# A wider gate on one load, a second bank for the last output tile, and one query tile turned a unit earlier, in a fused attention and feed-forward kernel

## The chip, the cores and the metric

The kernel runs on one core of a Trainium2 chip. The metric is the device time of one execution in microseconds (us). It was measured 13 times, and one execution was profiled. Times inside the kernel are counted from the first instruction of the profiled execution. PE is TensorE, DVE is VectorE, ACT is ScalarE, POOL is GpSimd, and SP is the engine that issues most of the DMA transfers.

## What is computed

Two stages follow each other. The first is a linear attention with a positional weight, over 8 batches of 8 heads, 576 positions and 64 channels:

```
phi(x) = concat(relu(x) * cos(theta_s), relu(x) * sin(theta_s))     # 64 -> 128 features
kv     = phi(k)^T v            z = sum_s phi(k)                      # per batch and head
x      = phi(q) kv / (phi(q) z + 1e-6)                               # attention output
```

The output is laid out as 4608 tokens of 512 channels and goes into a gated feed-forward block with 1536 hidden channels:

```
out = (gelu(x @ w_gate) * (x @ w_val)) @ w_out
```

All inputs and the output are float32. The kernel multiplies in bfloat16.

## The kernel before

**Stages and tiles.** The whole order is written out by hand: each engine carries out its own instructions in the order in which the program names them, and waits are put in where two instructions touch the same data or the same bank of PSUM. Positions of a batch are spread over the partitions so that a load is two transfers. `load` (L75) first issues the odd partitions (1, 3, ... 127; 4 positions each), then the even ones (0, 2, ... 126; 5 positions each):

```
for i, (s, r0, n) in enumerate(((1, 5, 4), (0, 0, 5))):
    (even if even and i == 1 else nc.sync).dma_start(
        out=dst[s:128:2, h0:h1, 0:n]..., in_=runs[:, :, r0:r0 + n]...)
```

For a whole batch the odd transfer of q is 512 KB and the even one 640 KB. There is one buffer each for raw q, k and v (`qf`, `kf`, `vf`), so the load of the next batch waits until the current one has been scaled into `qp`, `kp` and `vx`.

**Attention of a batch.** `sq` and `sk` scale q and k (ACT or DVE), `q_by_pe` turns a tile of q on PE, `kv_half` forms kv for four heads, `numer` (L190) multiplies one tile of 128 queries (8 matmuls into two banks) and normalises the result on DVE (`norm`: three instructions). `x_by_pe` (L318) then turns the normalised tile by 4 PE transposes into one bank, and ACT or DVE copies it into `xT`, the feed-forward input.

**Feed-forward.** `gv_unit(n, jt, c0, w, gb, vb)` (L209) does hidden tile `jt` of block `n` for `w` tokens from `c0`: 4 gate matmuls into bank `gb`, the gelu on ACT, 4 value matmuls into bank `vb`, and the product on DVE into `hT`. Block 0 is batch 0; blocks 1 to 8 hold 512 tokens each. `o_tile` multiplies 128 tokens of `hT` with `w_out` (12 matmuls into one bank), and ACT copies the result out for the store.

**Weights.** They are float32 in memory and are cast on their way by transfers that POOL issues. The first pair, hidden tiles 0 and 1 of gate and value (`load_w(0, 2)`, L345), is issued once batch 0's q has landed; tiles 2 and 3, 4 to 7 and 8 to 11 follow, then the two halves of `w_out` (L406, L407). After these, in the order of the program, stands a one-element copy by POOL (L408), and behind it the loads of batch 1 (`load_q(1)`, L409, and k and v). The copy reads the last element of the first half of `w_out` and writes an element of `qf`: it can only run once that half has landed, and a load that writes the same element has to wait for the copy.

**The start of block 1.** While the last output tiles of block 0 are multiplied, batch 1's attention tiles y0 to y4 are formed, turned, and given to the first two hidden tiles in pieces of 128, 128 and 256 tokens (L460 to L475). The piece of 256 tokens reads query tiles 2 and 3.

**The end.** The last of the 36 output tiles is done by `o_last` (L257) in two halves of 256 columns. For each half there are 12 matmuls; ACT copies the first 128 columns and DVE the second 128 (L267, L268), and SP and ACT issue one store each (L269, L270). It is called with bank 5.

Of the kernel before, what the change touches and what calls it, by code (L numbers as in the profile page):

```python
# [16 lines left out]
def kernel(  # L17
# [10 lines left out]
    nc = tc.nc  # L28
# [4 lines left out]
    C = H * D  # L33
# [24 lines left out]
    wo_sb = sb.tile([128, JT, C], BF16, name="wo_sb")  # L58
    xT = sb.tile([128, CT, N_TOK], BF16, name="xT")
    qf = sb.tile([128, H, NJ + 1, D], FP32, name="qf")  # L60
# [104 lines left out]
    def numer_mm(b, t, bank, g):  # L165
        for h in range(4 * g, 4 * g + 4):
            nc.tensor.matmul(  # L167
                ps[:, bank + g, (h % 4) * (D + 1):(h % 4 + 1) * (D + 1)],
                lhsT=qT[b % 2][:, t, h, :],
                rhs=kv[b % 2][:, h, 0:D + 1],  # L170
                start=True, stop=True,
            )

    def norm(xb, bank, g0, g1):

        n = g1 - g0
        nd = ps[:, bank + g0:bank + g1, 0:4 * (D + 1)].rearrange("p g (h e) -> p g h e", e=D + 1)
        den = rot.tile([128, 2, 4], FP32, name="den")
        nc.vector.tensor_scalar(den[:, 0:n], nd[:, :, :, D], EPS, None, op0=ALU.add)
        rec = rot.tile([128, 2, 4], FP32, name="rec")  # L180
        nc.vector.reciprocal(rec[:, 0:n], den[:, 0:n])
        nc.vector.tensor_tensor(  # L182
            xb[:, g0:g1], nd[:, :, :, 0:D],
            rec[:, 0:n, :, None].to_broadcast([128, n, 4, D]), op=ALU.mult,
        )

    def new_xb():
        return rot.tile([128, 2, 4, D], BF16, name="xb", bufs=4)

    def numer(b, t, bank):  # L190

        numer_mm(b, t, bank, 0)
        numer_mm(b, t, bank, 1)
        xb = new_xb()
        norm(xb, bank, 0, 2)
        return xb
# [12 lines left out]
    def gv_unit(n, jt, c0, w, gb, vb, mid=()):  # L209

        p0 = starts[n] + c0
        for ct in range(CT):
            nc.tensor.matmul(  # L213
                ps[:, gb, 0:w], lhsT=wg_sb[:, ct, jt * 128:(jt + 1) * 128],
                rhs=xT[:, ct, p0:p0 + w], start=(ct == 0), stop=(ct == CT - 1),
            )
        gel = rot.tile([128, 512], FP32, name="gel", bufs=3)
        nc.scalar.activation(gel[:, 0:w], ps[:, gb, 0:w], AF.Gelu)  # L218
        for f in mid:
            f()  # L220
        for ct in range(CT):
            nc.tensor.matmul(  # L222
                ps[:, vb, 0:w], lhsT=wv_sb[:, ct, jt * 128:(jt + 1) * 128],
                rhs=xT[:, ct, p0:p0 + w], start=(ct == 0), stop=(ct == CT - 1),
            )
        nc.vector.tensor_mul(hT[n % 2][:, jt, 64 + c0:64 + c0 + w], gel[:, 0:w], ps[:, vb, 0:w])  # L226
# [6 lines left out]
    def rows_ap(P, n):  # L233

        b, r = divmod(P, S)
        j, p0 = divmod(r, 128)
        rows = out[b * S:(b + 1) * S, :].rearrange("(i r) c -> i r c", r=9)
        if j < NJ:
            return rows[p0 // 2:(p0 + n) // 2, j:j + 6:5]
        return rows[:, NJ]  # L240
# [16 lines left out]
    def o_last(m, bank):  # L257

        c0 = 128 * m - starts[NB - 1] + 64
        o_sb = rot.tile([128, C], FP32, name="o_sb", bufs=4)  # L260
        for c in (0, 256):
            for jt in range(JT):
                nc.tensor.matmul(  # L263
                    ps[:, bank, c:c + 256], lhsT=hT[(NB - 1) % 2][:, jt, c0:c0 + 128], rhs=wo_sb[:, jt, c:c + 256],
                    start=(jt == 0), stop=(jt == JT - 1),
                )
            nc.scalar.copy(o_sb[:, c:c + 128], ps[:, bank, c:c + 128])  # L267
            nc.vector.tensor_copy(o_sb[:, c + 128:c + 256], ps[:, bank, c + 128:c + 256])  # L268
            nc.sync.dma_start(out=rows_ap(128 * m, 64)[:, :, c:c + 256], in_=o_sb[0:64, c:c + 256])  # L269
            nc.scalar.dma_start(out=rows_ap(128 * m + 64, 64)[:, c:c + 256], in_=o_sb[64:128, c:c + 256])  # L270
# [23 lines left out]
    def load_q(b):  # L294
        load(qf, q, b)
# [22 lines left out]
    def x_by_pe(b, t, xb, bank, eng, c0=0, c1=CT):  # L318
        p0 = b * S + t * 128
        cp = nc.vector.tensor_copy if eng == "v" else nc.scalar.copy  # L320
        xb2 = xb.rearrange("p g h d -> p (g h d)")
        view = ps[:, bank, 0:256].bitcast(BF16).rearrange("p (c t) -> p c t", c=CT)
        for ct in range(c0, c1):
            nc.tensor.transpose(out=view[:, ct], in_=xb2[:, ct * 128:(ct + 1) * 128], identity=ident)
        if t < NJ:
            cp(xT[:, c0:c1, p0:p0 + 128], view[:, c0:c1])  # L326
        else:
            cp(xT[:, c0:c1, p0:p0 + 64], view[:, c0:c1, 0:128:2])
# [76 lines left out]

    nc.gpsimd.dma_start(out=wo_sb[:, 0:6], in_=wo_r[:, 0:6])  # L406
    nc.gpsimd.dma_start(out=wo_sb[:, 6:12], in_=wo_r[:, 6:12])  # L407
    nc.gpsimd.tensor_copy(qf[0:1, 0, 0, 0:1], wo_sb[0:1, 5, C - 1:C])  # L408
    load_q(1)  # L409
    load_k(1)  # L410
    load(vf, v, 1, 0, 4)
# [55 lines left out]
    gv_unit(1, 1, 0, 128, 1, 5)  # L467
    x_by_pe(1, 2, y2, 6, "s")
    gv_unit(1, 0, 128, 128, 0, 4)
    gv_unit(1, 1, 128, 128, 1, 5)  # L470
    x_by_pe(1, 3, y3, 7, "s")
    y4 = numer(1, 4, 2)
    gv_unit(1, 0, 256, 256, 0, 4)
    x_by_pe(1, 4, y4, 6, "v")
    gv_unit(1, 1, 256, 256, 1, 5)  # L475
# [56 lines left out]
    for i, m in enumerate(last[:-1]):  # L532
        o_tile(NB - 1, m, 4 + i % 2)
    o_last(last[-1], 4 + (len(last) - 1) % 2)


# [28 lines left out]
```

## Time and profile before

| | us |
|---|---|
| median of 13 runs | 339.25 |
| lowest and highest of them | 335.4, 340.86 |
| the profiled execution's own time | 340.41 |
| its span, first to last instruction | 338.4 |
| PE busy in the span | 321.0 (95%) |
| DVE, ACT, POOL busy | 177.3, 149.8, 21.5 |
| mean granted PE clock | 0.988 |

The profile gives each engine's busy time, the same in 40 equal slices of the span, the busy share of the DMA engines, the waits (which engine at which line waited for whom, in total, how often, and the longest), the timeline, and the chain of work that ended last. "DMA share" can pass 1, since packets of different queues overlap on an engine. A PE that reads as busy isn't always at full rate: the granted clock is a row of its own.

### The profile page before, as it was taken

How to read it: one execution, taken by the hardware profiler on the slowest of the kernel's cores; microseconds unless marked ns; L12 is line 12 of the kernel's file. 1: busy time of each engine (PE TensorE's matmuls, PEld its weight loads, DVE VectorE, ACT ScalarE, POOL GpSimd, SP SyncE). 2: the span in 40 equal slices, each digit the busy share in tenths (PEclk: the TensorE clock that was granted, in tenths of full speed). 3: DMA queues.
4: the chain of work that ended last, by engine and by line, in shares of the span. 5: the costliest groups of instructions: out<-in, count | busy, mean ns of one | idle time of the engine just before them, and what ended most of it. 6: DMA issues, size and time to landing. Idle time of an engine off the chain costs nothing.

```text
span 338.4 us, 5911 instructions
## 1 busy us (share of the span) xinstructions
PE 321.0 (95%) x2225; PEld 172.7 (51%) x2260; DVE 177.3 (52%) x394; ACT 149.8 (44%) x275; POOL 21.5 (6%) x39
## 2 busy tenths in 40 slices
PE   7758999999999999999999999999999999999994
PEld 3546886665444544454445444544454444444443
DVE  4835459776766456645764576457645323222210
ACT  5834448775355325532553256225622332322321
POOL 2550001000010001000100010001000100000000
PEclk9969999999999999999999999999999999999999
DMA  7899984999939992997299829991914121000024
GB/s 232 236 206 207 233 290 120 363 197 351 164 61 159 369 182 48 198 370 164 42 225 367 138 44 195 374 174 32 202 35 75 32 62 33 31 31 33 32 63 93
DMA packets 84380, 54.65 MB, mean 162 GB/s; under 512 B 49408, under 2 KB 79872, under 8 KB 84352
## 3 DMA queue, kind: packets, MB, share of 16 engines
q1 hardware_dynamic: 78128, 49.10, 58.4%
q0 software_dynamic: 5792, 4.72, 8.8%
q10 hardware_dynamic: 432, 0.46, 0.4%
q8 instruction: 17, 0.28, 0.3%
q14 instruction: 11, 0.09, 0.1%
HBM read 37.75 MB, written 9.44 MB: 139 GB/s over the span
## 4 chain that ended last, share of the span: by engine, by line
PE 82%; DVE 6%; DMA 4%; issue 2%; ACT 2%; POOL 1%; SPq 1%; DVEq 0%; ACTq 0%; POOLq 0%
PE ps L245 27%; PE ps L213 25%; PE ps L222 24%; DVE vx L138 3%; PE ps L167 2%; DMA wv_sb<-in_moe_w_val_dram 2%; PE ps L151 2%; DMA qf<-in_q_dram 2%; DVE hT L226 1%; DVE xb L182 1%; PE ps L310 1%; PE ps L263 1%; ACT kp L134 1%; POOL wg_sb L291 1%; ACT xT L326 1%
## 5 line engine op out<-in xcount | busy, mean ns | idle before, releaser
L226 DVE TENSOR_TENSOR hT<-gel,ps 128x512 bf16<-128x512 f32 (+4 forms) x128 | 77.0, 603 | 135.1 <-PE ps L222 128.0
L213 PE MATMUL ps<-xT,wg_sb 128*128 128x512 bf16 (+5 forms) x498 | 114.1, 347 | 4.7 <-ACT xT L326 1.7
L222 PE MATMUL ps<-xT,wv_sb 128*128 128x512 bf16 (+5 forms) x500 | 112.8, 348 | 2.0 <-DMA wv_sb<-in_moe_w_val_dram 1.9
L218 ACT ACTIVATE gel<-ps 128x512 f32<-128x512 f32 (+4 forms) x128 | 67.8, 530 | 89.4 <-PE ps L213 86.6
L245 PE MATMUL ps<-wo_sb,hT 128*128 128x512 bf16 x413 | 95.3, 379 | 0.6
L222 PEld LDWEIGHTS <-wv_sb 128*128 128x128 bf16 x512 | 49.5, 99 | 47.3 <-DMA wv_sb<-in_moe_w_val_dram 2.1
L213 PEld LDWEIGHTS <-wg_sb 128*128 128x128 bf16 x512 | 47.4, 99 | 43.7 <-issue 2.5
L245 PEld LDWEIGHTS <-hT 128*128 128x128 bf16 x420 | 40.2, 98 | 45.8
L274 ACT COPY o_sb<-ps 128x512 f32<-128x512 f32 x35 | 20.5, 585 | 75.9 <-PE ps L245 71.7
L182 DVE TENSOR_TENSOR xb<-ps,rec 128x512 bf16<-128x512 f32 (+1 forms) x41 | 27.8, 678 | 1.5
L134 ACT ACTIVATE kp<-kf,sin_c 128x512 bf16<-128x512 f32 (+1 forms) x41 | 25.3, 679 | 0.9 <-DMA kf<-in_k_dram 0.9
L132 DVE TENSOR_SCALAR qp<-qf,cos_c 128x512 bf16<-128x512 f32 (+1 forms) x45 | 21.0, 511 | 0.8 <-DMA qf<-in_q_dram 0.8
L167 PEld LDWEIGHTS <-qT 128*128 128x128 bf16 x320 | 15.4, 99 | 8.8 <-issue 1.8
L134 ACT ACTIVATE qp<-qf,sin_c 128x512 bf16<-128x512 f32 (+1 forms) x30 | 18.8, 670 | 0.3 <-DMA qf<-in_q_dram 0.3
L132 DVE TENSOR_SCALAR kp<-kf,cos_c 128x512 bf16<-128x512 f32 (+1 forms) x45 | 18.0, 452 | 1.5 <-DMA kf<-in_k_dram 1.5
L167 PE MATMUL ps<-kv,qT 128*128 128x65 bf16 x320 | 17.1, 195 | 0.9 <-DVE kv L163 0.2
L206 POOL COPY xT<-xr 128x256 bf16<-128x256 bf16 x6 | 2.4, 400 | 205.7 <-DMA xr<-xb 205.7
L151 PEld LDWEIGHTS <-kp 128*128 128x128 bf16 x320 | 11.1, 97 | 3.5 <-issue 2.3
L151 PE MATMUL ps<-vx,kp 128*128 128x65 bf16 x320 | 11.9, 193 | 0.5
L138 DVE CAST vx<-vf 128x1280 bf16<-128x1280 f32 (+1 forms) x14 | 12.1, 892 | 0.3 <-DMA vf<-in_v_dram 0.3
L124 PE MATMUL ps<-junk 128*128 128x512 bf16 x30 | 9.5, 462 | 1.8 <-DVE par_i L101 1.7
L231 POOL COPY hT<-hT 128x768 bf16<-128x768 bf16 x8 | 7.6, 946 | 42.6 <-DVE hT L226 42.6
(53 smaller groups left out, 94.0 us busy)
## 6 DMA issues: line engine op xcount, KB each, us to landing
out_dram<-o_sb SPq DMA_DIRECT2D x38, 128.0 KB, 2.4
qf<-in_q_dram SPq DMA_DIRECT2D x7, 640.0 KB, 6.1
kf<-in_k_dram SPq DMA_DIRECT2D x7, 640.0 KB, 7.6
out_dram<-o_sb SPq DMA_DIRECT2D x16, 256.0 KB, 2.9
vf<-in_v_dram SPq DMA_DIRECT2D x6, 640.0 KB, 9.5
qf<-in_q_dram SPq DMA_DIRECT2D x7, 512.0 KB, 5.1
kf<-in_k_dram SPq DMA_DIRECT2D x7, 512.0 KB, 6.6
vf<-in_v_dram SPq DMA_DIRECT2D x6, 512.0 KB, 8.4
```

What stands on the lines that cost most here:

```text
L132: nc.vector.tensor_scalar(d, s, col, 0.0, op0=ALU.mult, op1=ALU.max)
L134: nc.scalar.activation(d, s, AF.Relu, scale=col)
L138: cp(vx[b % 2][:, :, h0:h1, 0:D], vf[:, h0:h1].rearrange("p h j d -> p j h d"))
L151: nc.tensor.matmul(ps[:, bank, (h % 4) * (D + 1):(h % 4 + 1) * (D + 1)], lhsT=kp[:, j, h, :], rhs=vx[b % 2][:, j, h, 0:D + 1], start=(j == ...
L167: nc.tensor.matmul(ps[:, bank + g, (h % 4) * (D + 1):(h % 4 + 1) * (D + 1)], lhsT=qT[b % 2][:, t, h, :], rhs=kv[b % 2][:, h, 0:D + 1], sta ...
L182: nc.vector.tensor_tensor(xb[:, g0:g1], nd[:, :, :, 0:D], rec[:, 0:n, :, None].to_broadcast([128, n, 4, D]), op=ALU.mult,)
L213: nc.tensor.matmul(ps[:, gb, 0:w], lhsT=wg_sb[:, ct, jt * 128:(jt + 1) * 128], rhs=xT[:, ct, p0:p0 + w], start=(ct == 0), stop=(ct == CT - 1),
L218: nc.scalar.activation(gel[:, 0:w], ps[:, gb, 0:w], AF.Gelu)
L222: nc.tensor.matmul(ps[:, vb, 0:w], lhsT=wv_sb[:, ct, jt * 128:(jt + 1) * 128], rhs=xT[:, ct, p0:p0 + w], start=(ct == 0), stop=(ct == CT - 1),
L226: nc.vector.tensor_mul(hT[n % 2][:, jt, 64 + c0:64 + c0 + w], gel[:, 0:w], ps[:, vb, 0:w])
L245: nc.tensor.matmul(ps[:, bank, :], lhsT=hT[n % 2][:, jt, c0:c0 + 128], rhs=wo_sb[:, jt, :], start=(jt == 0), stop=(jt == JT - 1),)
L274: nc.scalar.copy(o_sb, ps[:, bank, :])
```

## The change

Three edits. In `o_last`, the bank grows by `c // 128`, so the first 256 columns stay in bank 5 and the second 256 go to bank 7. The POOL copy ahead of batch 1's loads writes and reads two partitions in place of one, so that it touches partition 0 (which the even transfer of q writes) and partition 1 (which the odd one writes). And in the written order of block 1, the unit of hidden tile 1 for the second 128 tokens is put behind the turn of query tile 3 and the numerator of tile 4.

```diff
@@ o_last
         for c in (0, 256):
+            bank += c // 128
             for jt in range(JT):
                 nc.tensor.matmul(
                     ps[:, bank, c:c + 256], lhsT=hT[(NB - 1) % 2][:, jt, c0:c0 + 128], rhs=wo_sb[:, jt, c:c + 256],
@@
     nc.gpsimd.dma_start(out=wo_sb[:, 0:6], in_=wo_r[:, 0:6])
     nc.gpsimd.dma_start(out=wo_sb[:, 6:12], in_=wo_r[:, 6:12])
-    nc.gpsimd.tensor_copy(qf[0:1, 0, 0, 0:1], wo_sb[0:1, 5, C - 1:C])
+    nc.gpsimd.tensor_copy(qf[0:2, 0, 0, 0:1], wo_sb[0:2, 5, C - 1:C])
     load_q(1)
     load_k(1)
@@
     x_by_pe(1, 2, y2, 6, "s")
     gv_unit(1, 0, 128, 128, 0, 4)
-    gv_unit(1, 1, 128, 128, 1, 5)
     x_by_pe(1, 3, y3, 7, "s")
     y4 = numer(1, 4, 2)
+    gv_unit(1, 1, 128, 128, 1, 5)
     gv_unit(1, 0, 256, 256, 0, 4)
     x_by_pe(1, 4, y4, 6, "v")
     gv_unit(1, 1, 256, 256, 1, 5)
```

## The prediction

> **What bounds the kernel now.** I read the page first: engine rows, slices, chain; then the waits of PE in three stretches, the queues' packets there, and the timeline around the three edits. Engine busy time, and slices of 8.46 us:
>
> ```profile
> PE 321.0 (95%) x2225; PEld 172.7 (51%) x2260; DVE 177.3 (52%) x394; ACT 149.8 (44%) x275; POOL 21.5 (6%) x39
> ...
> PE   7758999999999999999999999999999999999994
> ...
> PEclk9969999999999999999999999999999999999999
> ...
> PE 82%; DVE 6%; DMA 4%; issue 2%; ACT 2%; POOL 1%; SPq 1%; DVEq 0%; ACTq 0%; POOLq 0%
> ```
>
> PE is the bound from the fourth slice to the last but one, and its matmuls are untouched, so only its holes can give time. The third slice (16.9 to 25.4 us) is the odd one: PE at 5 tenths, its clock at 6. PE's waits in 14 to 26 us, then (last line) its only wait for another engine in 64 to 74 us (us in total, times, longest):
>
> ```profile
> PE ps L222 <- DMA wv_sb<-in_moe_w_val_dram: 1.9, 1, 1.9
> PE ps L213 <- DMA wg_sb<-in_moe_w_gate_dram: 1.4, 1, 1.4
> ...
> PE ps L213 <- ACT xT L326: 0.7, 2, 0.4
> ```
>
> PE has nothing but the first gate and value weights to wait for: 3.3 us in all. The windows of one us there (window, length, PE busy, PEld, DVE, ACT, POOL, granted clock, DMA share, GB/s):
>
> ```profile
> 17.00:18.00 1.00, 0.84 (x12) 0.42 (x10) 0.37 (x2) 0.64 (x3) 0.66 (x2) 1.00 1.30 240
> 18.00:19.00 1.00, 0.00 (x0) 0.00 (x0) 0.93 (x3) 0.52 (x2) 1.00 (x3) 1.00 1.46 196
> ...
> 21.00:22.00 1.00, 0.40 (x4) 0.40 (x5) 0.00 (x0) 0.00 (x0) 0.43 (x2) 0.50 1.45 196
> ```
>
> The hole also costs clock: full at 18, half by 20. Other windows of that answer show half until 26, 0.77 in 26 to 27 and full after, so about 6.8 us at half, of which PE works from 21.6 on. The queues' packets in 17 to 18 us (first two lines) and in 18 to 20 us (third):
>
> ```profile
> q0 software_dynamic: 228, 0.12, 84.6%
> q1 hardware_dynamic: 131, 0.12, 45.7%
> ...
> q0 software_dynamic: 769, 0.38, 141.1%
> ```
>
> q0 carries the weights, q1 SP's loads. In 17 to 18 us half of the bytes that moved were not weights. They belong to the one load SP issued since 9 us, at 13.19 us, which landed 5.3 us later: the odd partitions of batch 1's q (512 KB). Its even half and all behind it stood until the POOL copy of L408 (38.2 us):
>
> ```profile
> SPq L78 <- POOL qf L408: 24.4, 1, 24.4
> ```
>
> Last, the tail: the second half of the last tile waits for VectorE's copy of the first.
>
> ```profile
> 332.51 0.29 DVE L268 COPY o_sb<-ps 128x128 f32<-128x128 f32 x1 [8.73 <-ACT o_sb L267]
> 332.83 2.68 SPq L269 DMA_DIRECT2D out_dram<-o_sb  x2
> 332.83 0.55 ACTq L270 DMA_DIRECT2D out_dram<-o_sb  x1
> 332.85 1.47 PE L263 MATMUL ps<-wo_sb,hT 128*128 128x256 bf16 x12 [0.72 <-DVE o_sb L268]
> ```
>
> **What the Trainium skill says.** "PSUM — Partial Sum Buffer", PSUM bank collisions: two engines must be kept apart by bank and quadrant, disjoint columns don't help. The trace agrees: ScalarE, VectorE and PE work on different columns of bank 5 and run one after the other (332.21, 332.51, 332.85). "DMA: Bandwidth & Descriptors", Queues, rings and completion order: each DMA engine takes turns between the queues it has work for, packet by packet. The two lines of 17 to 18 us agree: both queues move bytes. "TensorE: Matmul & The Clock Gate", Part 1: the clock halves after an idle window of about 3.4 us and returns after a busy one, and the windows run free of the kernel. Agrees: half from 19.6 to 26.5 us, two windows. "SBUF — State Buffer", Two separate sides: VectorE's fast copies can keep GpSimd from writing DMA descriptors. Consistent only: the first weight issue took 2.59 us (the next three 0.75 to 0.88) with VectorE busy.
>
> **Part 1, the last tile.** The second half's 12 matmuls go to bank 7, last used by batch 7's attention, long drained. Removed: the wait of 0.72 us. Nothing is added; the four copies and four stores stay. PE starts the second half at 332.13 instead of 332.85; ScalarE's second copy follows at 333.64, long after VectorE's first copy (to 332.80), and the SP issue at about 334.26, after the first store's issue (332.83 + 0.6). So the end moves by the whole wait: **-0.7 us** (bounds -0.75 and -0.6).
>
> **Part 2, the gate.** The POOL copy writes two partitions instead of one (0.17 us, at no one's cost: POOL's next work is the carry at 52 us). Moved: one SP issue (0.6 us) and its 512 KB, from 13.2 us to the release behind the first half of w_out. On SP nothing stands between but what already waited.
> *Early side.* Loads alone move about 365 GB/s (42 to 46 us: 1.46 MB in 4 us), so 0.52 MB cost 1.44 us of all DMA engines. Not all of it delays weights: up to 16.4 us q0 had hardly a packet ready (1 up to 16 us, 71 in 16 to 17) and the engines weren't full. From 16.4 us on some 250 of the load's 528 packets moved (0.6 of the 191 in 16 to 17, 131 in 17 to 18, 6 after), worth 250/528 x 1.44 = 0.7 us. Part of the rest may count too: the odd load's own packets began about 1.3 us after its issue, the weights' nearly 2 us after theirs (14.02), perhaps because of it. If q0's slow start is its own (descriptors), the gain is 0. So wv lands earlier by 0 to 1.44 us; I take **-1.0**: 21.6 becomes 20.6. PE was free for it at 18.3, so all of that reaches the chain, and its next deadlines are loose: weights 2 and 3 landed at 22.9 and 24.1 for a use at 29.7; 4 to 7 at 26.7 and 29.2 for 36.0.
> *Clock.* Of the half-speed time, 4.9 us had PE work (21.6 to 26.5), worth about 2.4 us. With a hole of 2.3 us in place of 3.3 fewer windows count as idle and the next is busier: in this trace's phase, 19.6 to 23.0 us would hold some 2.5 us of work in place of 1.4, perhaps enough to bring the clock back one window sooner (worth 1.3: PE's pieces from 23.9 to 26.5 are then half as long). Because windows run free I count half: **-0.6** (0 to -2.4).
> *Late side.* q0 without the rival frees the gate at about 37.2 instead of 38.2. SP then issues the odd half, 0.6 us later the even half, then k and v. The odd half lands by about 43.5, the even by 45.5 (5.3 us measured, plus its share of 0.5 MB more), k and v at most 1 us later than before. Their readers: q at 49.7 (48.1 after the gains of this part), k at 52.9, v at 59.0. Cost **0**, with 2.6 us of margin; if that cover were gone, each us late would hold ScalarE and VectorE at the first batch-1 scaling and then PE at the q transposes.
>
> **Part 3, the order.** The 8 matmuls of the second 128-column unit (jt 1) pass the 4 transposes of tile 3 and 8 numerator matmuls. No DMA moves. Before: transposes at 69.94, ScalarE's evacuation of xT 70.36 to 70.94, and the 256-column gate matmul, which needs it, started 71.00 after 0.42 us. After: transposes at 69.49; ScalarE is busy with tile 2's evacuation and one gelu until 69.93, so it evacuates 69.93 to 70.51. PE has the numerators and the moved unit (to 70.41), then starts at 70.57: 0.43 sooner. Added wait: the moved unit's gelu runs behind that evacuation, and its product on VectorE behind y4's normalisation (to about 71.4); what is queued behind both (the next gelu, the next product) needs PE's next unit first, and PE needs bank 5 only at 72.1. Late next: y4 for the last transposes, at 71.38 for 71.37, a tie, so 0.1 may return. **-0.35** (-0.45 to +0.1). The stage behind, ScalarE's five kp scalings (73.0 to 76.1), starts from the last gelu and moves along.
>
> **Sum.** -0.7 -1.0 -0.6 -0.35 = -2.65. The profiled execution took 340.41 (span 338.4 and 2.0 around it), which is high among the 13 runs (335.4 to 340.86, median 339.25): 337.8 for the like of it, **336.6** for the median, -0.8%.
>
> **Rivals.**
> *A, the weights' start is their own.* q0's ramp of packets looks much like a slow producer: 1, 71, 228 packets in three stretches, while POOL wrote descriptors until 16.4. For it: that ramp and the 2.59 us issue. Against: engines full from 16.5 on, with 45.7% q1. Then only parts 1 and 3: -1.05, 338.2, within 0.5%.
> *B, the hole nearly closes.* The first weight packet comes an us sooner and no window counts as idle: -0.7 -0.35 -1.44 -2.4 = -4.9, 334.4. For it: q0 in 16 to 18 us moved 0.16 MB where it moves 0.38 in the next 2 us. Against: PE would still wait 1.9 us.
> *C, the late side is not hidden: slower.* Batch 1's q lands after its reader. Place: first scalings at 48.1. It begins to cost when q's even half lands later than that, 2.6 us beyond my estimate, and eats the whole gain of 2.65 at 50.8; slower by over 0.5% (1.7 us) needs 52.5. For it: 0.5 MB more between 37 and 49 us, DMA share 1.0 to 1.28. Against: in the trace before, the last v load landed by 49.4, behind everything. At a landing of 53: about 341.5.
> *D, a part does not act.* The gate could miss the odd half still. The copy now touches partition 1, which the odd load writes, and the load waits for it; so I give this next to nothing.
>
> **Chances.** My case 0.60 (range 335.3 to 337.5), B 0.15, A 0.20, C 0.05. 0.5% is 1.7 us, about what a measurement of this kernel can tell from no change. Faster by more: mine and B, and the rare rest of A, 0.76. Within: A, and a little of C, 0.19. Slower: 0.05. Range: from near B's end to A's with the runs' own spread, 334.2 to 338.8.
>
> **What would show it.** Tail: PE's second half with no wait for VectorE. Gate: no q load between 9 and 36 us, SP's wait for POOL on the first of the pair, q0 at 140% share before 18 us, wv's wait for PE under 1 us; half clock ending before 26. Order: the wait for xT under 0.2 us near 70.5. I am wrong if wv's wait stays at 1.9, or if scalings wait for qf near 48.

## The result, and the profile after

The changed kernel takes 334.98 us (median of 11 runs, 333.74 to 338.02) against 339.58 for the kernel before (48 runs): 4.6 us or 1.4% less. The ratio of the two is 0.99, interval 0.9867 to 0.9933; it leaves out runs more than 1.5% above the fastest of their kernel, which the medians keep. A later repetition gave 334.86 against 339.31, ratio 0.9872 (0.9839 to 0.9905). The profiled execution took 337.16, so it is one of the longer ones.

The page of the changed kernel, the rows that answer to those of before:

```profile
PE 320.7 (96%) x2225; PEld 172.0 (51%) x2260; DVE 177.3 (53%) x394; ACT 149.7 (45%) x275; POOL 21.5 (6%) x39
...
PE   7868999999999999999999999999999999999995
...
PEclk9979999999999999999999999999999999999999
```

The third slice is still the odd one, with less of a hole (PE 6, clock 7). The waits of PE in 14 to 26 us (first line) and in 60 to 72 us (second):

```profile
PE ps L222 <- DMA wv_sb<-in_moe_w_val_dram: 2.3, 1, 2.3
...
PE ps L213 <- ACT xT L327: 0.2, 1, 0.2
```

The wait for wg is gone and the wait for wv has grown from 1.9 to 2.3: PE now stands still once for the first weights, where it stood still twice, 2.3 us in all in place of 3.3. Of the two waits for xT (0.7) one of 0.2 is left, at 66.36, two units ahead of the moved one; it stood in the kernel before as well. The wait of 0.42 at which the third edit aimed is gone. The windows of one us, columns as before, and the queues in 17 to 18 us:

```profile
17.00:18.00 1.00, 0.88 (x15) 0.63 (x14) 0.34 (x2) 0.63 (x3) 0.94 (x3) 1.00 1.15 135
19.00:20.00 1.00, 0.00 (x0) 0.00 (x0) 0.00 (x0) 0.00 (x0) 1.00 (x2) 1.00 1.38 176
20.00:21.00 1.00, 0.68 (x11) 0.69 (x12) 0.18 (x1) 0.00 (x0) 1.00 (x3) 0.88 1.38 175
24.00:25.00 1.00, 1.00 (x16) 0.83 (x13) 0.55 (x2) 0.43 (x2) 0.00 (x0) 0.91 1.26 209
...
q0 software_dynamic: 243, 0.12, 107.8%
```

The clock is half from 20.8 to 24.2 us: one window in place of two. There is no q1 line in 17 to 18 us any more, so the odd load has left; but only 135 GB/s move there, nearly all on q0, and I had expected it to fill the engines. SP issues both halves of batch 1's q once the gate opens, and nothing waits for them:

```profile
37.52 1.37 SPq L78 DMA_DIRECT2D qf<-in_q_dram  x2
```

The tail, from the timeline of the last 10 us:

```profile
328.25 2.78 PE L264 MATMUL ps<-wo_sb,hT 128*128 128x256 bf16 x24
...
330.11 0.29 DVE L269 COPY o_sb<-ps 128x128 f32<-128x128 f32 x1 [8.73 <-ACT o_sb L268]
...
331.07 0.27 ACT L268 COPY o_sb<-ps 128x128 f32<-128x128 f32 x1 [1.00 <-PE ps L264]
```

All 24 matmuls run as one group and VectorE's first copy lies beside them.

The two profiled executions can be laid side by side by the start of the same instruction:

| point in the program | before | after | gained since the point above |
|---|---|---|---|
| first value matmul | 21.61 | 20.32 | 1.29 |
| numerator of tile 3 (y3), L167 | 67.21 | 65.26 | 0.66 |
| first gate matmul of 512 columns | 72.97 | 70.57 | 0.45 |
| end of the last matmul | 334.32 | 331.04 | 0.88 |

The sum is 3.28, and the spans differ by 3.3. The pair is thus told by the four terms of the forecast: the landing of the weights, the clock, the order and the tail, each a little larger than forecast. Of the 1.29, 0.33 is not the gate's: in this execution POOL issued wv at 13.69, in that of before at 14.02. The medians moved by 1.3 more than this pair; the experiments are mostly about that.

### The profile page after: what moved, and what is told of

Its sections match the earlier page's. It is cut to its first block, busy times and chain, and to the rows that moved or that the text cites. A ratio compares the mean times of both kernels' runs of the same rounds, so it can differ in the third digit from the quotient of the medians.

```text
span 335.1 us, 5911 instructions
## 1 busy us (share of the span) xinstructions
PE 320.7 (96%) x2225; PEld 172.0 (51%) x2260; DVE 177.3 (53%) x394; ACT 149.7 (45%) x275; POOL 21.5 (6%) x39
## 4 chain that ended last, share of the span: by engine, by line
PE 83%; DVE 6%; DMA 4%; issue 2%; ACT 2%; POOL 1%; SPq 1%; DVEq 0%; POOLq 0%; ACTq 0%
PE ps L245 27%; PE ps L213 25%; PE ps L222 25%; DVE vx L138 3%; PE ps L167 3%; DMA wv_sb<-in_moe_w_val_dram 2%; PE ps L151 2%; DMA qf<-in_q_dram 2%; DVE hT L226 1%; DVE xb L182 1%; PE ps L311 1%; PE ps L264 1%; ACT kp L134 1%; POOL wg_sb L292 1%; SPq L78 1%
## 5 line engine op out<-in xcount | busy, mean ns | idle before, releaser
L167 PEld LDWEIGHTS <-qT 128*128 128x128 bf16 x320 | 15.4, 99 | 9.1 <-issue 1.8
L167 PE MATMUL ps<-kv,qT 128*128 128x65 bf16 x320 | 17.1, 195 | 1.2 <-DVE qT L317 0.4
```

The costliest lines, as they stand in the source:

```text
L167: nc.tensor.matmul(ps[:, bank + g, (h % 4) * (D + 1):(h % 4 + 1) * (D + 1)], lhsT=qT[b % 2][:, t, h, :], rhs=kv[b % 2][:, h, 0:D + 1], sta ...
```

## Experiments

`dummies(n, 5)` writes n matmuls of 512 columns from a buffer of zeros to bank 5. Whole-kernel times are medians; the kernel before was at 339.90 beside the first four, at 339.31 beside the next four, and at 339.59 beside the last four.

**The gate alone.**

```diff
-    nc.gpsimd.tensor_copy(qf[0:1, 0, 0, 0:1], wo_sb[0:1, 5, C - 1:C])
+    nc.gpsimd.tensor_copy(qf[0:2, 0, 0, 0:1], wo_sb[0:2, 5, C - 1:C])
```

> Only the two-partition gate, from the kernel before. Clock theory (the median gained more than forecast because the shorter hole often leaves the clock at full, worth 2.4 us and not 0.6): 3.2 to 3.6 us faster than before, with several runs at a mean clock of 0.999 or 1.0. Rival (the weights landed much earlier than forecast, clock as forecast): 1.6 to 2 us faster at most, clock 0.99 in all runs. Rival (the gain sits in the other two edits): under 1 us. In the trace: no wait for wg, wv's wait about 2.3 us ending near 20.4.

336.79, 3.1 us faster; ratio 0.9934 (0.9907 to 0.9961). Its profiled execution kept full clock throughout. The first value matmuls, from the timeline:

```profile
19.14 0.40 PE L222 MATMUL ps<-xT,wv_sb 128*128 128x128 bf16 x4 [0.83 <-DMA wv_sb<-in_moe_w_val_dram]
```

wv comes at 19.14 in this run and 20.32 in the changed kernel's, though POOL issued it within 0.15 us of the same time: issue to landing took 5.5 us and 6.6 us. Without the gate it was 7.5 in the kernel before. The gain is just under the 3.2 to 3.6 of the clock theory, but the earlier landing takes part in it; the table of starts further down splits the two.

**The other two edits without the gate.**

```diff
+            bank += c // 128                     # in o_last
@@
-    gv_unit(1, 1, 128, 128, 1, 5)
     x_by_pe(1, 3, y3, 7, "s")
     y4 = numer(1, 4, 2)
+    gv_unit(1, 1, 128, 128, 1, 5)
```

> The bank and the order edit without the gate. Clock theory: 0.72 + 0.45 = 1.2 us faster than before, its clock spread like that of before, wv's wait ending near 21.6 as before. Rival (the gain sits in these two): 2.5 us or more.

337.91, 2.0 us faster; ratio 0.9944 (0.9918 to 0.9971). More than 1.2, so the expectation missed; a table below shows that among runs with one or two windows at half speed the gain is 1.3, and that the rest goes with the mix: 6 of these 22 runs had two windows, against 35 of 56 of the kernel before. Why, the runs don't tell. The median also hides two groups: 17 of its 22 runs lie at 337.1 to 338.9 and five at 334.35 to 335.9. Its profiled execution is the fastest of all, and its first weight issue shows why. POOL's and VectorE's lines of that execution, from the timeline:

```profile
11.45 0.90 POOL L292 DMA_DIRECT2D wg_sb<-in_moe_w_gate_dram  x1 [8.71 <-ACT wg_sb L345]
...
11.82 0.62 DVE L132 TENSOR_SCALAR qp<-qf,sin_c 128x256 bf16<-128x256 f32 x1
12.36 1.10 DVE L132 TENSOR_SCALAR qp<-qf,cos_c 128x256 bf16<-128x256 f32 x3
```

The same in the changed kernel:

```profile
11.12 2.58 POOL L292 DMA_DIRECT2D wg_sb<-in_moe_w_gate_dram  x1 [8.40 <-ACT wg_sb L345]
...
11.91 0.35 DVE L132 TENSOR_SCALAR qp<-qf,sin_c 128x256 bf16<-128x256 f32 x1
...
13.88 0.56 DVE L138 CAST vx<-vf 128x640 bf16<-128x640 f32 x1 [0.36 <-DMA vf<-in_v_dram]
```

Read the durations against each other. Where VectorE's scalings run at their usual 0.35, POOL's issue takes 2.58 and ends at 13.70, 0.18 us after VectorE first stands still (13.88 - 0.36 = 13.52). In all eight other profiles with a long issue it ends 0.17 to 0.19 us after that moment too. Where POOL takes 0.90, a VectorE scaling takes 0.62 in place of 0.35. This fits the exclusive port of the Trainium skill ("SBUF — State Buffer", Two separate sides: whichever of the two starts first keeps the shared pair, and the other blocks). The runs show that each delays the other; that the port is the reason is the page's explanation, and why POOL got in amid the scalings here they don't tell. With the short issue the first weights are under way at 14 us, before the odd q load, and PE waits for no weight at all.

**Keeping the clock up by dummies.**

```diff
+    dummies(6, 5)                                # kernel before only
-    gv_unit(0, 0, 0, 128, 0, 1)
+    gv_unit(0, 0, 0, 128, 0, 1, (lambda: dummies(8, 5),))   # 9 in the changed kernel
```

> The kernel before, with 6 dummy matmuls (512 columns, onto bank 5) ahead of the first gate matmuls and 8 between them and the first value matmuls, so that PE is busy while it waits for weights. No data moves otherwise. Clock theory: the half-speed time goes, about 2.4 us faster than before (near 337), clock 1.0 in all runs and a much smaller spread. Rival (clock unimportant): within 0.5 us of before.

> The changed kernel, with 9 dummy matmuls between the first gate and the first value matmuls. Clock theory: all runs at clock 1.0 and near the fastest runs of the changed kernel, 333.8 to 334.2, and 2.2 to 2.6 us below the kernel before with dummies (the tail 0.72, the order 0.45, the weights 1.0 to 1.4). Rival (clock unimportant): as the changed kernel, 335.0, with its spread of 4 us.

The kernel before with dummies: 338.10, 1.8 us faster (ratio 0.9973, 0.9953 to 0.9992), less than the 2.4 expected; 18 of 22 runs lie within 337.7 to 338.4. PE in this kernel, from the timeline:

```profile
20.10 1.89 PE L124 MATMUL ps<-junk 128*128 128x512 bf16 x8
21.83 0.39 PE L222 MATMUL ps<-xT,wv_sb 128*128 128x128 bf16 x4
```

The first value matmuls come right behind the dummies and no sooner than before (21.61). So what this kernel gains lies behind them, where PE's pieces now run at full clock. The dummies also hide when the weights come: in the profile of the bank edit below wv landed near 19.1 and its first value matmuls still came at 21.69. That the spread is smaller is therefore not the clock's doing alone.

The changed kernel with dummies: 335.81, which is slower than without. That expectation failed: the dummies occupy PE until 19.7, and after_again below shows wv at 19.26. The difference of the two is 2.29, within the 2.2 to 2.6 expected, but it is in part the difference between 14 dummies and 9, and what it leaves beside the tail and the order is no measure of the gate.

**Where each trace gains.** The points of the table above, each trace against that of the kernel before:

| trace | up to the first value matmul | from there to y3 | to the first gate matmul of 512 columns | to the end |
|---|---|---|---|---|
| changed | 1.29 | 0.66 | 0.45 | 0.88 |
| changed, again | 2.35 | 0.69 | 0.45 | 0.88 |
| gate alone | 2.47 | 1.89 | 0.01 | 0.00 |
| before with dummies | -0.22 | 1.90 | 0.01 | 0.00 |
| the same with the bank edit | -0.08 | 1.89 | 0.01 | 0.86 |
| the same with the order edit | 0.32 | 1.89 | 0.45 | 0.00 |

The order and the tail stand where their edits are, and nowhere else. The second column goes with the clock behind the first value matmul: 1.9 us where both half-speed windows of before are gone, whether gate or dummies did it, and 0.7 where one is left. So in these traces the gated kernels gain 1.3 to 2.5 us at the landing and 0.7 to 1.9 by the clock.

**The mean clock of every run** tells about how many windows at half speed it had: one window (20.8 to 24.2 us in the changed kernel's trace, 3.4 us) is worth 1.7 of 335 us, or 0.5%. The profiled runs agree: 0.988 has two, 0.994 one, 1.0 none. (The profiled runs are counted in.)

| kernel | two windows (to 0.990) | one (0.992 to 0.996) | none (from 0.997) |
|---|---|---|---|
| before | 35 runs, 340.14 | 15, 339.14 | 6, 336.23 |
| bank and order | 6, 338.83 | 12, 337.79 | 4, 335.54 |
| gate alone | 0 | 7, 337.96 | 8, 336.34 |
| changed | 0 | 7, 336.79 | 5, 334.12 |

No run with the gate has two windows, and about half have none. The columns can't be read as the price of a window alone: the clock doesn't tell when the weights came, nor where the window lay. In the profiles of after_yield, of the kernel before with dummies and of its bank edit, the only window lies at 11.3 to 14.7 us, ahead of the weights. For the windows in and behind the hole, the profiles without dummies go in order: PE stood still for weights 5.1 us in the run "More beside the first weights" below (three windows), 3.3 in before (two), 2.3 in the changed kernel, 1.7 in the run "The late side" and 1.2 in after_again (one each), 0.8 in gate alone and not at all in those with a short issue (none). So few traces give no threshold.

**The changed kernel again.**

> The changed kernel unaltered, to see how its runs fall into modes. The traces so far show two durations of POOL's first weight issue: 2.4 to 2.6 us (ending just when VectorE first idles, near 13.5 to 14.0) and 0.90 us (in bank_and_order's profile, where VectorE's scalings were held instead, and PE then waited for no weight at all). Port theory: which of the two engines comes first is chance and not touched by the change; so runs cluster near 333.8 (short issue) and at 335 to 337.2 (long issue, clock varying), and kernel before at 335.4 and 339 to 340. Rival (the change itself makes the short issue likelier): well over a third of these runs at 333.7 to 334.3 again, with hardly any of before at 335.4 on the same chip. Rival (one mode, only the clock differs): no run below 334.5 at a clock under 1.0 and none above 335 at 1.0.

334.86; four runs at 334.4 to 335.0 with full clock, two at 336.0 and 337.3 with one window. On this chip none of 14 runs of before was under 338. The profiled execution had the long issue (2.56) and wv at 19.26. The port theory doesn't fit: there was no group at 333.8. The last rival (one mode, only the clock differs) fits these six runs, and the first series too if a clock from 0.997 counts as full. Whether the five quickest runs of the first series (333.7 to 334.3) had the short issue can't be said, as no trace of them exists.

**Letting POOL go first.** A one-element copy on POOL, and one on VectorE that needs it, ahead of the second half of q's scalings.

```diff
+            nc.gpsimd.tensor_copy(tiny[0:1, 2:3], wg_sb[0:1, 0, 0:1])
+            nc.vector.tensor_copy(tiny[0:1, 3:4], tiny[0:1, 2:3])
             load_w(0, 2)
```

> The changed kernel, with a one-element copy by POOL ahead of the first weight issue and a one-element copy of its result by VectorE ahead of the second half of q's scalings: VectorE stands still for about 0.5 us just when POOL starts its issue. Port theory: the first issue takes 0.9 us in the profile, no wait for wv over 0.5 us, clock at full, and all runs within 0.6 us of each other near 334 to 334.6. Rival (the duration of the issue has another cause): 2.4 to 2.6 us as before, times as the changed kernel's or 0.5 us slower.

> The same two one-element copies in the kernel before. Port theory: weights are under way before batch 1's odd q load can hinder them, so the gate's share of the change nearly vanishes: about 335.5 to 336, 4 us below the kernel before, and only 1.2 to 1.7 us above after_yield (tail 0.72, order 0.45, up to 0.5 for the gate). Rival (the gate's gain is independent of the issue): 2.5 us or more above after_yield.

The kernel before: 336.10, that is 3.2 us faster by two tiny copies (ratio 0.9901, 0.9874 to 0.9928). The changed kernel: 334.92, the same as without them; above the 334 to 334.6 expected, and from 334.8 to 336.2 in place of within 0.6. POOL and PE in the changed kernel with them, from the timeline:

```profile
11.33 0.90 POOL L292 DMA_DIRECT2D wg_sb<-in_moe_w_gate_dram  x1 [0.30 <-POOL tiny L346]
...
18.58 0.64 PE L213 MATMUL ps<-xT,wg_sb 128*128 128x128 bf16 x4
19.06 0.39 PE L222 MATMUL ps<-xT,wv_sb 128*128 128x128 bf16 x4
```

Issues of 0.90 and 1.00, no wait for a weight in either kernel. The two differ by 1.18, which leaves nothing for the gate beside the tail and the order, and the first value matmuls come at 18.81 in the kernel before and 19.06 in the changed one. So the gate, worth 3.1 us in the median of its own experiment, whose trace has the long issue, is worth nothing that shows when the first weights start early: the odd load can only hinder what it meets. The changed kernel gains nothing, for PE reaches the first unit at 18.58 in place of 17.43. VectorE, held by POOL, is later with the work ahead; but this execution also had its half-speed window there, so the 1.15 us are not split between the two. The kernel before with the copies, at full clock, reaches it at 18.34.

**The bank alone and the order alone**, each in the kernel before with dummies, where the spread is small.

> The bank edit alone, in the kernel before with the 14 dummy matmuls (before_warm: 338.1, spread 0.7 without four runs). My tail: 0.72 us below before_warm, 337.4. Rival (the end is set by the first half's stores or the closing wait, not by PE): 338.1.

> The order edit alone, in the kernel before with the 14 dummy matmuls (before_warm 338.1). My step: 0.35 to 0.45 us faster, 337.7, PE's wait for xT in the first units of block 1 gone. Rival (the time is given back behind it, in ScalarE's five kp scalings): 338.1, with a longer wait for a gelu near 76.

337.26 and 337.59 against 338.10, thus 0.84 and 0.51 faster. Both agree with the table of starts (0.88 and 0.45), and both rivals fall. The three were timed on different chips. The medians of the kernel before differ there by up to 0.6, but those of its runs with two windows by 0.13 (340.14 to 340.27), so the difference is mostly their mix. The sizes rest on the table of starts.

**More beside the first weights.** The gate moved behind both halves of q.

```diff
-    nc.gpsimd.tensor_copy(qf[0:1, 0, 0, 0:1], wo_sb[0:1, 5, C - 1:C])
     load_q(1)
+    nc.gpsimd.tensor_copy(kf[0:2, 0, 0, 0:1], wo_sb[0:2, 5, C - 1:C])
```

> The kernel before with the gate moved behind batch 1's q and onto kf: both halves of q (1.15 MB in place of 0.5) load beside the first weights. Dose theory (what SP loads beside the first weights delays them by at least its own time): at 365 GB/s the 0.64 MB more cost 1.75 us, so with a long first issue wv's wait ends near 23.4 and the runs are 1.7 to 3 us slower than before, 341 to 343; runs with a short issue stay near 336. Rival (the odd half matters by its place in time, not by its bytes): same as before, 339.5.

342.04, 2.45 us slower (ratio 1.0072, 1.0046 to 1.0099), all four runs at a clock of 0.985 to 0.989. PE's first units from the timeline:

```profile
19.23 0.61 PE L213 MATMUL ps<-xT,wg_sb 128*128 128x128 bf16 x4 [1.80 <-DMA wg_sb<-in_moe_w_gate_dram]
23.10 0.60 PE L222 MATMUL ps<-xT,wv_sb 128*128 128x128 bf16 x4 [3.26 <-DMA wv_sb<-in_moe_w_val_dram]
```

wv took 9.5 us from issue to landing. With 0.52 MB beside it and a long issue it took 7.5, 7.6 and 7.9 (three traces), with none 5.5 to 6.7 (five, 6.1 on average). So 0.52 MB cost about 1.6 us and the next 0.64 MB about 1.8, near their own time at 365 GB/s (1.44 and 1.75), though single traces differ by more. Dose theory fits, with one trace at the large dose, and the half-speed stretch grew to three windows there (19.3 to 29.5).

**The late side.** The gate reads the second half of w_out.

```diff
-    nc.gpsimd.tensor_copy(qf[0:2, 0, 0, 0:1], wo_sb[0:2, 5, C - 1:C])
+    nc.gpsimd.tensor_copy(qf[0:2, 0, 0, 0:1], wo_sb[0:2, 11, C - 1:C])
```

> The changed kernel with the gate reading the second half of w_out in place of the first: batch 1's q, k and v are released about 3.5 us later (near 41 us). It tests the cover on the late side. My estimate (q's even half has 2.6 us to spare) says: q lands about 1 us after its reader would start, so 0.5 to 1.5 us slower than the changed kernel (335.4 to 336.4), with a wait of ScalarE or VectorE for qf near 48. Rival (more cover than I thought): same as the changed kernel, 334.9, no such wait.

336.31 of four runs (335.32 to 337.04); the changed kernel's own runs spread as widely, so the time decides nothing. The timeline does:

```profile
48.70 0.72 ACT L134 ACTIVATE qp<-qf,sin_c 128x512 bf16<-128x512 f32 x1 [0.94 <-DMA qf<-in_q_dram]
48.73 0.48 DVE L132 TENSOR_SCALAR qp<-qf,cos_c 128x512 bf16<-128x512 f32 x1 [0.29 <-DMA qf<-in_q_dram]
```

Issued at 41.1 in place of 37.5, q is late by 0.9. That did not reach PE: from the first value matmul to y3 it took 44.9 us, as in the changed kernel's trace, so the cost that I expected isn't shown. In the changed kernel the even half landed at about 44.4 (issued near 38.3, 6.1 us to landing) for a reader at 47.8: 3.4 us of cover, and no wait.

**An attempt at a faster version.** after_yield with weights 2 and 3 loaded later.

```diff
             load_w(0, 2)
@@
-    load_w(2, 4)
@@
+    load_w(2, 4)
     load_w(4, 8)
```

> after_yield (334.92), with the loads of weights 2 and 3 issued after those of 0 and 1 by some 5 us (just ahead of 4 to 7). In after_yield's profile VectorE's scalings and casts between 11.7 and 14.8 us are stretched by about 1.3 us while POOL issues four weight loads in a row; PE then reaches the first unit at 18.6 instead of 17.4. Port theory: with two issues in place of four VectorE loses about half of that, 0.4 to 0.7 us faster than after_yield, 334.2 to 334.5. Rival (VectorE's delay has another source, or is hidden): 334.9.

335.71: slower than after_yield. PE did get its first value weights sooner (18.19 against 19.06), but weights 2 and 3 came later, q was issued at 39.3 in place of 36.7, and the late side took it back (first value matmul to y3: 45.2 us against 44.0), as the timeline shows:

```profile
46.73 0.72 ACT L134 ACTIVATE qp<-qf,sin_c 128x512 bf16<-128x512 f32 x1 [1.96 <-DMA qf<-in_q_dram]
```

No version tried is clearly faster than the changed kernel.

## Why the prediction was right, step by step

- **Sign and range.** 334.98 lies in the range of 334.2 to 338.8, toward its lower end. But 336.6 was 1.6 us too high, and my own case (335.3 to 337.5, chance 0.60) missed too: the range held because it reached down to rival B.
- **A sign that misled.** I had named a wait for wv of 1.9 as the sign of being wrong, and one under 1 us as the sign of being right. It was 2.3, though the gate worked. I had overlooked that the wait for wg would vanish, so that the whole hole shows up at wv; the sum of the two (3.3 before, 2.3 after) was the thing to read. The sign on q0 failed as well (107.8% in 17 to 18 us, not 140%).
- **Part 1, the tail.** Forecast 0.7 (0.6 to 0.75), measured 0.88 in the traces and 0.84 between medians. PE's wait of 0.72 is gone; the remaining 0.16 is that the 24 matmuls take 2.78 in one group and took 1.47 each in two.
- **Part 3, the order.** Forecast 0.35, measured 0.45. ScalarE's evacuation ran at 67.97, so the gate matmul at 68.60 found it done; the tie over y4 cost nothing to speak of, and the kp stage behind moved along.
- **Part 2, the landing.** Forecast 1.0, with bounds from 0 to 1.44. The traces give 1.29 (changed), 2.35 (again: 19.26) and 2.47 (gate alone), of which 0.3 to 0.5 is that POOL issued earlier in these executions than in that of before (13.55 to 13.71, against 14.02). From issue to landing the gate saves 0.9 to 2.0 us against that execution. The term that was too small is the count of packets: I let only the 250 that moved after 16.4 us count, and the dose run fits the whole load. The bound of 1.44, the load's own time, was no bound for a single execution. What makes a gated landing vary between 5.5 and 6.7 us stays open.
- **Part 2, the clock.** Forecast 0.6, half of the 1.3 for one window. In the pair of profiles 0.66 came out, which is luck: one window did go, and it was worth half of what I had reckoned. Where both windows went it was 1.9, less than the 2.4 I gave as the most, but more than the 0.6 I took. Most runs of before (35 of 56) had two windows and no gated run had more than one. The direction was right (a shorter hole, less half-speed time), but the weight of one half was taken from one profile's phase.
- **Part 2, the late side.** Forecast as covered, with 2.6 us to spare; measured 3.4. Rival C needs q later by more than that: a wait of 0.9 for q (gate 3.6 us later) cost PE nothing, one of 2.0 (the attempt at a faster version) did.
- **Rival A** (the weights' slow start is their own) was right that the start is slow for a reason of its own, POOL's issue waiting for VectorE's first pause, and wrong to conclude that the odd load then costs nothing: it meets exactly the late start. **Rival B**, at 334.4, came nearer in time than my own case. Its clock came true in five of twelve runs, which had no window, and the 1.9 us of waiting that it left over lie within the 0.8 to 2.3 of the three gated traces. I had given it 0.15.

## What to carry to other kernels

A load that slips past its gate can cost more than its bytes suggest when it meets the transfer that PE waits for: with a longer hole came a longer time at half clock here, so look at the clock of all runs, not of one profile. When a gate protects one partition of a buffer that is loaded in two halves, check which half the gate's element belongs to. When a hole is expected to shrink, add up all the waits in it, for one of them can grow while the sum falls. And where GpSimd issues a transfer in the middle of a dense stretch of VectorE, read the duration of the issue: it can wait for VectorE's first pause.

## What the runs showed of the hardware that was not expected

- The issue of a weight load by POOL took 2.3 to 2.6 us beside back-to-back VectorE scalings and ended 0.17 to 0.19 us after their first pause; in other executions of like programs it took 0.90 and VectorE was held. Two one-element copies settled the order and were worth 3.2 us in the kernel before. Three traces with the copies show 0.90 to 1.00; nine without them show the long issue and two the short one.
- In the changed kernel's trace the first weight transfers, with no load of SP's beside them, moved only 129 to 170 GB/s between 15 and 19 us, where q0 later moved about 205. The runs don't tell why.
- The clock was at half for one, two or three stretches of 3.4 us, and taking two of them away behind the first value matmul was worth 1.9 us, once by the gate and three times by dummy matmuls that compute nothing.
